# One attention and mixture-of-experts kernel: key and query splitting of the first two batches on GpSimd alone

## The chip, the cores and the metric

The kernel runs on one core of one Trainium2 chip. The metric is the device time of one execution in microseconds; the median of several runs is compared. A core has five engines with queues of their own: TensorE (matrix products; its weight loads are shown apart), VectorE, ScalarE, GpSimd and SyncE, which here issues the loads and stores. In the profile they are called PE (PEld for weight loads), DVE, ACT, POOL and SP; SPq is SP's queue.

## The reference

All data are float32. Three layers follow one another on 4 batches of 576 tokens with 8 heads of 64:

```python
scores = (q @ k.T) / 8
thresh = max(scores) - tau
scores = where(scores >= thresh, scores, -1e9)
attn = exp(scores - max(scores)); attn /= sum(attn) + 1e-9
x = attn @ v                              # heads side by side: 576 x 512

h = x.T @ U @ V                           # 576 -> 32 -> 576, over tokens
u = x + h.T
x = u + relu(u @ w_ch1) @ w_ch2           # 512 -> 2048 -> 512

e = expert of each token                  # argmax of logits, or the previous token's
out = p[e] * (relu(x @ w1[e]) @ w2[e])    # 8 experts, 512 -> 1024 -> 512
```

## The kernel before

**Split operands.** The products that must be precise are made from pairs: a high part rounded to TensorE's reduced float32 form (`F32R`) and a low part, the difference to the full value. For scores, keys are two tiles, `kh` and `kl`. The queries lie twice on the 128 partitions: in `qs`, partitions 0 to 63 hold the high part of the scaled queries and partitions 64 to 127 the low part, so that one product with `kh` and one with `kl` give the score.

**Pairs.** Heads are worked in pairs, four to a batch, numbered `i = 4 b + hp`: pairs 0 to 3 are batch 0, pairs 4 to 7 batch 1. `load_pair` (L261) loads one pair's queries and keys in pieces ("cuts"): from the second pair on, keys of 576 and 640 columns, then queries of 608 and 608. Each cut comes from memory through SP into a tile `raw` of a ring of three (L281), is copied by ScalarE into the high part (L289 keys; L292 queries, with the scale 1/8 in `t8[:, 1:2]`), and the low part is a subtraction: keys on `eng` (L290), queries on VectorE over 64 partitions (L294). `eng` is VectorE for the very first pair and for batches 2 and 3, and GpSimd otherwise. The tiles `qs`, `kh`, `kl` exist twice, so a pair's parts can be written once the scores of the pair two before it are done.

**Batch 0 alone.** `attention_alone(0)` (L553) runs first. Each of its steps takes one score tile (128 queries by 576 keys): four score products (L313, L315), the maximum on VectorE (L348), the exponential on ScalarE (L359), the thresholds (L352) and the masking with the row sum on VectorE (L363). A pair has nine such tiles. Score tiles are two in number. Beside them run the older tiles' transposes on TensorE (L416) and their copies on ScalarE (L417), the products with the values (L435, L436) and the token mixing (`chain`, L447, with `inverse`, L378, on 128x4 row sums). A generator `conv` narrows the 64-bit weights: a load `cr` (L204), a cast on ScalarE (L212), a join on VectorE (L219) and a store (L243). The next pair's `load_pair` is started during the current pair's second group, one cut a step. On TensorE a few filler products (L585) fill short steps.

**Order of the queues.** In this stage GpSimd's instructions stay in the order of the program (`tc.manual_schedule` around `attention_alone(0)`, L855). The other queues' order is laid out ahead of time by a planner, from the program's order and its own estimates of durations; instructions of later calls, such as `load_w` (L664) with its subtraction on GpSimd (L681), can stand among those of this stage.

**Later.** Batches 1 to 3 run their attention interleaved with the 512-2048-512 layer of the batch before (`channel`, L725); its weights are split by `load_w`, in batch 0's layer largely on GpSimd (L678, L681). Routing and the experts follow.

Of the kernel before, what the change touches and what calls it, by code (L numbers as in the profile page):

```python
# [8 lines left out]
F32 = mybir.dt.float32  # L9
# [5 lines left out]
AF = mybir.ActivationFunctionType  # L15
ALU = mybir.AluOpType
# [87 lines left out]
def attention_channel_moe(ctx, tc, qk, vv, tau, umat, vrep, wch, wgl, wexp, consts, out):  # L104
    nc = tc.nc
    pe, dve, act, pool, sp = nc.tensor, nc.vector, nc.scalar, nc.gpsimd, nc.sync
# [10 lines left out]
    t8 = cp.tile([128, 4], F32, name="t8")  # L117
# [135 lines left out]
    def scalars():  # L253

        sp.dma_start(out=t8[:, 0:1], in_=tau)

        dve.tensor_scalar(out=t8[:, 1:2], in0=t8[:, 0:1], scalar1=NEGTAU, scalar2=0.125, op0=ALU.is_ge, op1=ALU.mult)
        dve.tensor_scalar(out=t8[:, 2:3], in0=t8[:, 1:2], scalar1=0.0, scalar2=BIG, op0=ALU.is_equal, op1=ALU.mult)
        dve.tensor_scalar(out=t8[:, 0:1], in0=t8[:, 0:1], scalar1=0.0, scalar2=t8[:, 2:3], op0=ALU.max, op1=ALU.add)

    def load_pair(b, hp, later=None):  # L261

        i = b * NPAIR + hp
        v = ap.tile([128, VW], F32, tag="v", name=f"v{i}")
        qs = ap.tile([128, QKW], F32R, tag="qs", name=f"qs{i}")
        kh = ap.tile([128, QKW], F32R, tag="kh", name=f"kh{i}")
        kl = ap.tile([128, QKW], F32R, tag="kl", name=f"kl{i}")

        cuts = ((0, 0, 128), (1, 0, S), (0, 704, 832), (1, S, QKW), (0, 128, 704), (0, 832, QKW)) if i == 0 else (
            (1, 0, S), (1, S, QKW), (0, 0, 608), (0, 608, QKW))  # L270
        eng = dve if i == 0 or b > 1 else pool
        def steps():
            for n, (kq, c0, c1) in enumerate(cuts):
                c = slice(c0, c1)
                nm = f"raw{i}_{n}"
                if (i, n) == (0, 1):
                    x = mlp.tile([128, S], F32, tag="yr", name=nm, bufs=2)
                elif i == 0 and c1 - c0 == 128:
                    x = mlp.tile([128, 512], F32, tag="wr", name=nm, bufs=WR)
                else:  # L280
                    x = ap.tile([128, 640], F32, tag="raw", name=nm, bufs=3)  # L281
                x = x[:, :c1 - c0]
                sp.dma_start(out=x, in_=qk[i][:, kq, c])
                if (i, n) == (0, 0):
                    scalars()
                if (i, n) == (0, 3):
                    sp.dma_start(out=cst, in_=consts)
                if kq:
                    act.activation(kh[:, c], x, AF.Copy)  # L289
                    eng.tensor_tensor(out=kl[:, c], in0=x, in1=kh[:, c].bitcast(F32), op=ALU.subtract)  # L290
                else:
                    act.activation(qs[:, c], x, AF.Copy, scale=t8[:, 1:2])  # L292
                    lo, hi, xl = qs[64:128, c], qs[64:128, c].bitcast(F32), x[64:128]
                    dve.scalar_tensor_tensor(out=lo, in0=xl, scalar=t8[64:128, 1:2], in1=hi,  # L294
                                             op0=ALU.mult, op1=ALU.subtract)
                yield
            sp.dma_start(out=v, in_=vv[i])

        if later is None:
            for _ in steps():  # L300
                pass
        else:
            later.append(steps())
        return qs, kh, kl, v
# [231 lines left out]
    def attention(b):  # L536
        prev = None
        nxt = load_pair(b, 0)
        for hp in range(NPAIR):
            inp = nxt  # L540
            if hp + 1 < NPAIR:
                nxt = load_pair(b, hp + 1)
            for g in range(5):
                fr = front(b, hp, g, inp)
                yield 1.0
                if prev is not None:
                    yield from with_chain(back(*prev))
                prev = (b, hp, g, inp, fr)
        yield from with_chain(back(*prev))
        while CHAIN:  # L550
            yield link()

    def attention_alone(b):  # L553

        pend, debt, loads = [], 0.0, []
        inps = {0: load_pair(b, 0)}
        seq = [(hp, g, h) for hp in range(NPAIR) for g in range(5) for h in range(1 if g == 4 else 2)]
        groups = {}
# [816 lines left out]
```

## Time and profile before

| what | value |
|---|---|
| median of 3 runs | 1031.87 us (1031.58 to 1033.2) |
| the profiled execution's own time | 1030.82 us |
| its span, first to last instruction | 1029.0 us |
| mean granted TensorE clock | 0.997 of full |
| busy: PE, DVE, ACT, POOL | 995.0, 719.4, 612.1, 153.7 us |

The span is that of one profiled execution; 1.8 us of its time lie outside it. Busy shares are means over stages that differ: batch 0's attention alone lasts to about 100 us, batch 1's attention with batch 0's layer to about 240 us, attention altogether to about 620 us.

### The profile page before, as it was taken

The page shows a single profiled execution, that of the slowest core. Times are in us where ns is not written, and L with a number is a line of the kernel's source. Part 1 is how long each engine was busy: PE and PEld are TensorE (multiplying, and loading weights), DVE is VectorE, ACT ScalarE, POOL GpSimd, SP SyncE. Part 2 cuts the span into 40 slices and gives each one's busy share as a digit, 9 for nine tenths or more (in the row PEclk, how much of TensorE's full clock was granted, in tenths as well). Part 3 has the DMA queues.
Part 4 walks back from the last instruction along what each step waited for, and adds up shares of the span by engine and source line. Part 5 has one row for each costly group of instructions (what it writes and reads, how often), then busy time and mean ns, then how long its engine had stood idle before and what let it go on. Part 6 is the DMA issues. An engine that isn't in the chain of part 4 may idle for free.

```text
span 1029.0 us, 17858 instructions
## 1 busy us (share of the span) xinstructions
PE 995.0 (97%) x6351; PEld 835.8 (81%) x6352; DVE 719.4 (70%) x1761; ACT 612.1 (59%) x1242; POOL 153.7 (15%) x143
## 2 busy tenths in 40 slices
PE   7898999989999999999999999999999999999996
PEld 4666677768787787788888898999998988889984
DVE  7898697876778877877676664683369755576673
ACT  6888777775677777776565653422354434455562
POOL 1332245342000000000000000013400321120100
PEclk9999999999999999999999999999999999999998
DMA  6655577864323322423121111453055555556650
GB/s 215 226 145 162 164 245 254 266 205 146 118 92 94 125 71 83 127 90 94 55 68 42 42 43 31 139 208 121 25 196 178 176 201 184 173 188 199 197 184 16
DMA packets 58241, 143.72 MB, mean 140 GB/s; under 512 B 7389, under 2 KB 8157, under 8 KB 58144
## 3 DMA queue, kind: packets, MB, share of 16 engines
q1 hardware_dynamic: 54784, 132.27, 40.2%
q0 software_dynamic: 3360, 10.23, 3.1%
q8 instruction: 52, 0.85, 0.3%
q14 instruction: 45, 0.37, 0.1%
HBM read 124.65 MB, written 18.61 MB: 139 GB/s over the span
## 4 chain that ended last, share of the span: by engine, by line
PE 78%; ACT 6%; DVE 5%; DMA 5%; issue 3%; POOL 1%; SPq 0%; POOLq 0%; DVEq 0%; ACTq 0%
PE l L717 6%; PE l L719 6%; PE l L718 6%; PE l L702 6%; PE l L703 6%; PE l L704 6%; PE tp L416 4%; PE po L435 4%; PE el L1194 3%; PE el L1195 3%; PE el L1196 3%; PE s L313 3%; PE s L315 3%; PE el L1241 3%; PE el L1239 3%
## 5 line engine op out<-in xcount | busy, mean ns | idle before, releaser
L1125 ACT ACTIVATE eh<-ew 128x512 fp32r<-128x512 f32 x160 | 94.2, 628 | 67.9 <-PE el L1241 45.3
L1126 DVE TENSOR_TENSOR el<-ew,eh 128x512 fp32r<-128x512 f32 x160 | 106.6, 692 | 37.7 <-ACT eh L1125 36.3
L702 PE MATMUL l<-uh,w0h 128*128 128x256 f32 (+2 forms) x352 | 127.0, 361 | 0.3 <-ACT yT L508 0.3
L363 DVE SCALAR_TENSOR_TENSOR p<-s,st,p 128x576 f32<-128x576 f32 x144 | 114.2, 815 | 16.7 <-ACT p L359 13.1
L359 ACT ACTIVATE p<-s,st 128x576 f32<-128x576 f32 x144 | 103.8, 739 | 32.6 <-DVE st L348 31.3
L703 PE MATMUL l<-ul,w0h 128*128 128x256 f32 (+2 forms) x352 | 122.6, 348 | 0.0
L704 PE MATMUL l<-uh,w0l 128*128 128x256 f32 (+2 forms) x352 | 122.2, 347 | 0.0
L348 DVE TENSOR_REDUCE st<-s 128x1 f32<-128x576 f32 x144 | 105.2, 750 | 17.0 <-PE s L315 16.5
L717 PE MATMUL l<-hh,w1h 128*128 128x512 f32 (+3 forms) x320 | 115.2, 360 | 0.0
L719 PE MATMUL l<-hh,w1l 128*128 128x512 f32 (+3 forms) x320 | 112.9, 353 | 0.0
L718 PE MATMUL l<-hl,w1h 128*128 128x512 f32 (+3 forms) x320 | 112.2, 351 | 0.0
L417 ACT ACTIVATE ptt<-tp 128x512 f32<-128x512 f32 (+1 forms) x192 | 88.7, 491 | 30.2 <-PE tp L416 30.0
L313 PE MATMUL s<-kh,qs 128*128 128x288 f32 x320 | 95.4, 318 | 5.4 <-DVE p L363 3.5
L681 POOL TENSOR_TENSOR w1l<-wr,w1h 128x512 fp32r<-128x512 f32 x24 | 31.8, 1337 | 457.0 <-DVE rha L984 426.7
L416 PE MATMUL tp<-cst,p 128*128 128x128 f32 x576 | 90.8, 276 | 5.2 <-ACT ptt L417 5.0
L722 DVE TENSOR_TENSOR yT<-l,yT 128x448 f32<-128x448 f32 (+2 forms) x96 | 50.1, 522 | 57.9 <-PE l L719 57.5
L315 PE MATMUL s<-kl,qs 128*128 128x288 f32 x320 | 88.5, 297 | 0.0
L373 ACT ACTIVATE p<-p,rv 128x576 f32<-128x576 f32 x108 | 78.6, 771 | 16.1 <-DVE rv L380 16.0
L416 PEld LDWEIGHTS tp<-cst,p 128*128 128x128 f32 x576 | 67.8, 140 | 20.4 <-ACT ptt L417 11.4
L313 PEld LDWEIGHTS s<-kh,qs 128*128 128x128 f32 x320 | 60.3, 188 | 15.5 <-DVE p L363 6.4
L706 DVE SCALAR_TENSOR_TENSOR hl<-l,hh 128x512 fp32r<-128x512 f32 (+2 forms) x80 | 46.3, 579 | 36.7 <-ACT hh L705 36.4
L702 PEld LDWEIGHTS l<-uh,w0h 128*128 128x128 f32 x352 | 66.5, 189 | 6.8 <-DVE rsm L797 0.7
(604 smaller groups left out, 2473.0 us busy)
## 6 DMA issues: line engine op xcount, KB each, us to landing
ew<-in_wexp_dram SPq DMA_DIRECT2D x80, 512.0 KB, 4.6
wr<-wdram SPq DMA_DIRECT2D x128, 256.0 KB, 3.1
cr<-in_wch_dram SPq DMA_DIRECT2D x32, 512.0 KB, 5.1
raw<-in_qk_dram SPq DMA_DIRECT2D x30, 304.0 KB, 3.2
wdram<-w SPq DMA_DIRECT2D x32, 256.0 KB, 3.0
v<-in_vv_dram SPq DMA_DIRECT2D x16, 352.0 KB, 4.1
raw<-in_qk_dram SPq DMA_DIRECT2D x16, 320.0 KB, 3.6
raw<-in_qk_dram SPq DMA_DIRECT2D x17, 288.0 KB, 3.3
```

The costliest lines, as they stand in the source:

```text
L313: pe.matmul(s["t"][:, h, :288], lhsT=qs[:, qc:qc + 128], rhs=kh[:, k0:k0 + 288], start=(j == 0), stop=False)
L315: pe.matmul(s["t"][:, h, :288], lhsT=qs[:, qc:qc + 128], rhs=kl[:, k0:k0 + 288], start=False, stop=(j == n - 1))
L348: dve.tensor_reduce(out=self.st[:, 0, h:h + 1], in_=self.t[h], axis=AX.XY, op=ALU.max, negate=True)
L363: dve.scalar_tensor_tensor(out=p, in0=self.t[h], scalar=self.st[:, 1, h:h + 1], in1=p, op0=ALU.is_ge, op1=ALU.mult, accum_out=self.rvs[:, ...
L416: pe.transpose(tp[:, c - c0], src[:, c * 128:c * 128 + 128], ident)
L702: pe.matmul(pm, lhsT=w1h[:, wk], rhs=uh[k], start=(k == 0), stop=False)
L703: pe.matmul(pm, lhsT=w1h[:, wk], rhs=ul[k], start=False, stop=False)
L704: pe.matmul(pm, lhsT=w1l[:, wk], rhs=uh[k], start=False, stop=(k == 3))
L717: pe.matmul(pm, lhsT=w2h[:, wd], rhs=xh, start=(f == f0), stop=False)
L718: pe.matmul(pm, lhsT=w2h[:, wd], rhs=xl, start=False, stop=False)
L719: pe.matmul(pm, lhsT=w2l[:, wd], rhs=xh, start=False, stop=(f == f0 + 3))
L1126: dve.tensor_tensor(out=lo, in0=x, in1=hi.bitcast(F32), op=ALU.subtract)
```

## The change

For pairs 1 to 7 the high parts of the keys are copied by GpSimd instead of ScalarE; their low parts were on GpSimd already. For pairs 1 to 3 GpSimd takes the queries as well: it scales the raw cut in place, copies it into the high part, and subtracts on the 64 lower partitions. Pair 0 and the queries of pairs 4 to 7 stay as they were, and so do batches 2 and 3.

```diff
         eng = dve if i == 0 or b > 1 else pool
+        own = eng is pool
...
                 if kq:
-                    act.activation(kh[:, c], x, AF.Copy)
+                    if own:
+                        pool.tensor_copy(kh[:, c], x)
+                    else:
+                        act.activation(kh[:, c], x, AF.Copy)
                     eng.tensor_tensor(out=kl[:, c], in0=x, in1=kh[:, c].bitcast(F32), op=ALU.subtract)
+                elif own and b == 0:
+                    lo, hi, xl = qs[64:128, c], qs[64:128, c].bitcast(F32), x[64:128]
+                    pool.tensor_scalar(out=x, in0=x, scalar1=t8[:, 1:2], scalar2=None, op0=ALU.mult)
+                    pool.tensor_copy(qs[:, c], x)
+                    pool.tensor_tensor(out=lo, in0=xl, in1=hi, op=ALU.subtract)
                 else:
                     act.activation(qs[:, c], x, AF.Copy, scale=t8[:, 1:2])
                     lo, hi, xl = qs[64:128, c], qs[64:128, c].bitcast(F32), x[64:128]
```

## Rows read from the trace of the kernel before

**Rows 1.** The page: busy us, share of the span and instructions of each engine.
```profile
PE 995.0 (97%) x6351; PEld 835.8 (81%) x6352; DVE 719.4 (70%) x1761; ACT 612.1 (59%) x1242; POOL 153.7 (15%) x143
```
**Rows 2.** Busy time by stage: stretch, its length, busy us and instructions by engine, clock, DMA.
```profile
10.00:98.00 88.00, 75.82 (x529) 54.98 (x530) 80.57 (x194) 71.09 (x148) 24.34 (x20) 1.00 0.60 182
...
120.00:240.00 120.00, 114.56 (x689) 88.20 (x688) 95.43 (x193) 88.11 (x166) 49.48 (x48) 1.00 0.79 249
```
**Rows 3.** Waits of VectorE, 10 to 98 us: total us, times, longest.
```profile
DVE st L348 <- PE s L315: 3.4, 6, 1.2
DVE p L363 <- ACT p L359: 2.2, 3, 1.1
```
**Rows 4.** Waits of TensorE, 10 to 98 us.
```profile
PE tp L416 <- ACT ptt L417: 4.1, 6, 1.5
```
**Rows 5.** ScalarE's groups, 10 to 98 us: busy us, mean ns | idle before.
```profile
L292 ACT ACTIVATE qs<-raw,t 128x608 fp32r<-128x608 f32 x8 | 6.5, 810 | 1.6 <-DMA raw<-in_qk_dram 1.6
...
L289 ACT ACTIVATE kh<-raw 128x640 fp32r<-128x640 f32 x5 | 3.7, 739 | 0.7 <-DMA raw<-in_qk_dram 0.7
L289 ACT ACTIVATE kh<-raw 128x576 fp32r<-128x576 f32 x5 | 3.4, 681 | 1.4 <-issue 0.8 <-POOL w1l L681 0.6
```
**Rows 6.** VectorE in order of time: start us, duration us, instruction, idle before.
```profile
18.52 0.85 DVE L294 SCALAR_TENSOR_TENSOR qs<-raw,t,qs 64x608 fp32r<-64x608 f32 x1
...
38.68 0.82 DVE L363 SCALAR_TENSOR_TENSOR p<-s,st,p 128x576 f32<-128x576 f32 x1 [1.09 <-ACT p L359]
...
46.99 0.16 DVE L379 TENSOR_SCALAR rv<-rv 128x4 f32<-128x4 f32 x1
...
51.36 1.02 DVE L379 TENSOR_SCALAR rv<-rv 128x4 f32<-128x4 f32 x1
...
79.43 0.85 DVE L294 SCALAR_TENSOR_TENSOR qs<-raw,t,qs 64x608 fp32r<-64x608 f32 x1
```
**Rows 7.** ScalarE in order of time.
```profile
14.71 0.69 ACT L289 ACTIVATE kh<-raw 128x576 fp32r<-128x576 f32 x1
...
19.84 0.80 ACT L292 ACTIVATE qs<-raw,t 128x608 fp32r<-128x608 f32 x1 [0.35 <-DMA raw<-in_qk_dram]
...
37.22 0.80 ACT L292 ACTIVATE qs<-raw,t 128x608 fp32r<-128x608 f32 x1 [0.79 <-DMA raw<-in_qk_dram]
```
**Rows 8.** Waits of TensorE, 118 to 245 us.
```profile
PE tx L461 <- ACT yT L442: 2.7, 3, 1.1
```
**Rows 9.** VectorE's groups, 10 to 98 us.
```profile
L294 DVE SCALAR_TENSOR_TENSOR qs<-raw,t,qs 64x608 fp32r<-64x608 f32 x8 | 7.5, 935 | 0.3
...
L219 DVE SCALAR_TENSOR_TENSOR w<-cr,top 128x512 int32<-128x512 int32 x7 | 6.4, 912 | 0.0
L379 DVE TENSOR_SCALAR rv<-rv 128x4 f32<-128x4 f32 x8 | 3.8, 478 | 0.1
...
L219 DVE SCALAR_TENSOR_TENSOR wv<-crv,top 128x512 int32<-128x512 int32 x1 | 0.7, 684 | 0.0
```
**Rows 10.** GpSimd's groups, 10 to 98 us.
```profile
L290 POOL TENSOR_TENSOR kl<-raw,kh 128x640 fp32r<-128x640 f32 x5 | 8.2, 1647 | 0.1
L290 POOL TENSOR_TENSOR kl<-raw,kh 128x576 fp32r<-128x576 f32 x5 | 7.5, 1494 | 18.4 <-ACT kh L289 18.4
...
L678 POOL CAST w1h<-wr 128x512 fp32r<-128x512 f32 x1 | 0.6, 610 | 16.0 <-DMA wr<-wdram 16.0
```
**Rows 11.** TensorE in order of time.
```profile
28.61 0.38 PE L313 MATMUL s<-kh,qs 128*128 128x288 f32 x1
```
**Rows 12.** GpSimd in order of time.
```profile
51.06 1.28 POOL L681 TENSOR_TENSOR w1l<-wr,w1h 128x512 fp32r<-128x512 f32 x1 [2.01 <-ACT w1h L680]
```
**Rows 13.** SyncE's queue in order of time: DMA issues.
```profile
18.52 3.62 SPq L283 DMA_DIRECT2D raw<-in_qk_dram  x3
23.86 7.05 SPq L204 DMA_DIRECT2D cr<-in_wch_dram  x3
```
**Rows 14.** Waits of ScalarE, 10 to 98 us.
```profile
ACT top L212 <- DMA cr<-in_wch_dram: 0.2, 1, 0.2
```

## The prediction, made before the changed kernel was run

> **What bounds the kernel now.** I read the page first: TensorE is busy 97% of the span, VectorE 70%, ScalarE 59%, GpSimd 15% [rows 1]. That is an average over unlike stages, so the table of windows comes next [rows 2]. In the second attention stage (120 to 240 us) TensorE works 114.6 of 120 us and little is left to win. In the first batch's attention alone, which runs steadily from 10 to 98 us, VectorE is the fullest: 80.6 of 88 us (92%), TensorE 75.8 (86%), ScalarE 71.1 (81%), GpSimd 24.3 (28%). What VectorE waits for there is short: 3.4 us for scores and 2.2 us for the exponential [rows 3]; TensorE's longest wait is 4.1 us for ScalarE's copies of the transposed probabilities [rows 4]. So this stage is paced by VectorE, with ScalarE and TensorE close behind, and it is worth what VectorE's queue gets shorter, as long as the others can follow. Behind it lies TensorE work of a fixed size, so I let a gain of this stage arrive at the end whole.
>
> **Removed from ScalarE.** In the stage, ten key copies (five pairs, the next batch's first two among them) of 739 and 681 ns, 7.1 us, and six query copies of 810 ns, 4.9 us: 12.0 us, to 59 us [rows 5]. ScalarE is not the fullest engine, so I give this no price by itself; it shows only where ScalarE holds up others. At 37.22 a query copy stood 0.79 us at the head of ScalarE's queue for its load; the exponential behind it came late, and VectorE idled 1.09 us before its mask at 38.68 [rows 6, 7]. That wait goes to GpSimd's queue: minus 1.1 us. Shorter queues should trim TensorE's 4.1 us as well [rows 4], which come back as VectorE's 3.4 us for scores; I take 0.5 us. Four more key copies (pairs 6 and 7, 2.8 us) fall into 120 to 240 us, where TensorE's longest wait on ScalarE is 2.7 us in three pieces [rows 8]; I take nothing there, with 2.7 as the far end.
>
> **Removed from VectorE.** Eight query subtractions of 64x608 stand in the stage, 7.5 us [rows 9]; the two of pair 4 (the first at 79.43, 0.85 us) stay [rows 6], so six leave, 5.8 us.
>
> **Added to GpSimd.** A 128x512 cast there takes 0.61 us, a two-input subtraction 1.49 (576 columns) and 1.65 (640) [rows 10]. Scaled by columns, a key copy is 0.69 or 0.76 and a query copy 0.72; the query subtraction 1.57, taken as one of 608 columns, though it covers 64 partitions. A scaling with a per-partition factor has no row on GpSimd: from below the cast, 0.72, from above the two-input subtraction, 1.57. It reads one tensor, as the cast does, so I take 0.72. A query cut is then 3.0 us (3.9), a pair's keys 1.45 more. In the stage: 6 x 3.0 + 5 x 1.45 = 25.3 us, GpSimd from 24.3 to 49.6 of some 84 us (59%); it does not become the bound.
>
> **Is it in time?** Pair 1 is the tightest. Its first key copy stood at 14.71 and its last query load had landed by 19.84 [rows 7]. From 14.7 GpSimd's chain is 0.7 + 1.5 + 0.8 + 1.65 (19.3), first query cut 22.3, second 25.3 (27.1 with the dear scaling). TensorE's first scores of pair 1 start at 28.61 [rows 11]. Hidden, by 3 us and more; uncovered, each late microsecond would cost one on TensorE and so on all.
>
> **The shared reads.** VectorE's small 128x4 scaling took 0.16 us at 46.99, with GpSimd idle, but 1.02 at 51.36 [rows 6]: GpSimd's 1.28 us subtraction had begun at 51.06 and ended at 52.34, and VectorE's ended at 52.38 [rows 12]. It waited the other's instruction out. Groups hit so: the 128x4 scalings, 8 x (478 - 160) = 2.5 us, the two-input joins, 7 x (912 - 684) = 1.6, and the query subtractions, 8 x (935 - 850) = 0.7 [rows 6, 9]. The first two, 4.1 us, stay exposed. If VectorE arrives at a random moment it waits half of the instruction that it meets, so the sum grows with the squares of GpSimd's durations: now 24.7 us2 for ten key subtractions and about 12 for the other 8.6 us; added 5 for key copies, 21 for query cuts; over 84 instead of 88 us that is a factor 1.8. So 4.1 becomes 7.4: plus 3.3 us (plus 4.7 with the dear scaling; nothing, if arrivals happen to miss).
>
> The Trainium skill (SBUF — State Buffer, Who interferes with whom) calls the port pair of VectorE and GpSimd an exclusive lock: the later of the two blocks for the whole instruction if the VectorE one uses a 2-port mode or two SBUF inputs. The trace agrees with it in the 1.02 us above. A reader who left the lock out would book 5.8 + 1.1 + 0.5 = 7.4 us of gain; with it the sum is 4.1.
>
> **Sum.** Minus 5.8, plus 3.3, minus 1.1, minus 0.5: minus 4.1 us. The profiled execution took 1030.82 us (span 1029.0); the median of the runs is 1031.87, 1.05 above. So 1031.87 - 4.1 = 1027.8 us. What a measurement of this kernel can tell from no change is 0.2%, 2.1 us.
>
> **Rivals.**
> *Same: VectorE's freed time turns into waiting.* TensorE, at 75.8 of 88 us, could close in at once, and most of the net 2.5 us on VectorE would return as longer waits for the other two; also the dear scaling leaves only 5.8 - 4.7 + 1.6 = 2.7 us, and a little less is within the noise. Against: VectorE's waits for both others are 5.6 of 88 us now, ScalarE gets 12 us lighter and TensorE has 12 us of room [rows 2, 3]. Time 1031 (1030 to 1033).
>
> *Slower: VectorE waits out GpSimd.* The 15 exposed instructions wait 0.79 us each if they always meet a two-input GpSimd instruction at a random moment, which is 11.8 us and only eats the gain (1031.87 - 5.8 + 7.7 - 1.6 = 1032.2). If they become ready just as GpSimd starts, as at 51.36, where 0.86 of 1.28 us was waited, they wait up to 1.57 each. At 1.1 us, 16.5 in all, it is plus 12.4: 1031.87 + 12.4 - 7.4 = 1036.9 (1044 with all waits whole). Behind the waiting instruction stand maximum and mask, and behind them TensorE's next scores. It makes the kernel slower by 0.2% once the stalls pass 4.1 + 7.4 + 2.1 = 13.6 us. For it: GpSimd at 59%. Against: that is not always, and half of the added instructions are of some 0.7 us.
>
> *Slower: raw buffers held longer.* Three raw buffers feed SyncE's queue. Pair 2's three loads were issued over 3.6 us from 18.52 as buffers came free, and the three weight loads of the conversion stand right behind at 23.86 [rows 13]. GpSimd frees the first query buffer at 22.3, where VectorE did at 19.4 [rows 6]. Up to 3 us per pair could pass to the weight loads, whose casts sit in ScalarE's ordered queue before exponentials: 3 x 3 - 4.1 = 5 us slower, 1036.5, from the point where the casts' loads have no lead left. Against: ScalarE's wait on those loads is 0.2 us in the whole stage [rows 14].
>
> *Queues laid differently.* Only GpSimd's order is written out in this stage; subtractions of a later call already stand among the first batch's at 51.06 [rows 12]. A changed step can reorder the rest, by some 2 us either way; it is no part of the sum.
>
> *More than forecast.* If stalls don't grow and both of VectorE's waits shrink [rows 3]: minus 5.8 - 2.2 - 1 = 9, 1022.9.
>
> **How the numbers follow.** Forecast (2 to 7 us gained) 0.57; more than that 0.05; same 0.19; VectorE waiting out GpSimd 0.09; raw buffers 0.04; reordered to worse 0.06 (1034 to 1036). Faster by over 0.2%: 0.57 + 0.05 = 0.62; within: 0.19; slower: 0.19. The range takes in 1022.5 (the gain without stalls) and reaches to 1033.7 (just under what 0.2% calls slower, 1034); the forecast's own is 1024.5 to 1029.8.
>
> **What would show it.** Right: no query subtraction of pairs 1 to 3 on VectorE, GpSimd near 50 us busy in the stage, 128x4 scalings and joins with a mean near 0.6 and 1.0 us, pair 4's first scores some 4 us earlier, and the same lead at 240 us. A query scaling near 1.5 us would halve the gain. Wrong: TensorE waiting on GpSimd's query parts; ScalarE's casts waiting for weight loads; stalls over 13.6 us; or a lead after the stage that is gone at 240.

## The result and the profile after

The changed kernel is slower. Its median is 1044.53 us (1042.07 to 1047.67, four runs) against 1031.75 us for the kernel before on the same chip (1031.58 to 1033.2): a ratio of 1.0118, interval 1.0097 to 1.0139. The forecast was 1027.8, range 1022.5 to 1033.7; direction and range were both missed. The profiled execution took 1045.72 us, its span is 1043.7, 14.7 us more than before. Lines move by 1 to 9 after the change: L284 loads `raw`, L291 and L294 are the key copy and subtraction on GpSimd, L297 to L299 the three new query instructions, L682 loads the weights `wr`, L689 and L690 copy and subtract them.

The first line of the page, which answers to [rows 1]:

```profile
PE 1001.6 (96%) x6352; PEld 841.1 (81%) x6352; DVE 713.4 (68%) x1755; ACT 601.4 (58%) x1222; POOL 190.8 (18%) x175
```

The table of windows, with columns as in [rows 2]; the last two rows cut the first batch's stage finer:

```profile
10.00:98.00 88.00, 70.29 (x460) 50.80 (x461) 68.20 (x173) 55.69 (x117) 50.82 (x42) 0.94 0.56 176
66.00:76.00 10.00, 2.49 (x31) 1.93 (x29) 2.59 (x7) 1.85 (x7) 1.29 (x2) 0.79 0.54 173
76.00:86.00 10.00, 9.68 (x51) 7.60 (x52) 7.25 (x18) 6.89 (x15) 5.77 (x5) 0.70 0.36 91
```

VectorE's 80.6 us in the first stage became 68.2, so work left the fullest engine as intended, and GpSimd's 24.3 became 50.8, as worked out. But TensorE fell from 75.8 to 70.3: the stage did not run faster on a lighter VectorE, it did less in the same time. The row of 66 to 76 us says where: no compute engine was busy for more than 2.6 of 10 us.

How far each kernel is shows in the start of the first maximum of a pair's scores (VectorE's timeline, L348 before, L357 after) and of ScalarE's first copy into `uh` (after batch 0) and into `rest` (after batch 1), in us:

| kernel | pair 2 | pair 3 | pair 4 | after batch 0 | after batch 1 | span |
|---|---|---|---|---|---|---|
| before | 53.2 | 76.5 | 100.8 | 102.9 | 236.8 | 1029.0 |
| after | 50.3 | 83.4 | 109.5 | 112.8 | 248.7 | 1043.7 |
| after, pair 4's loads later | 50.7 | 76.7 | 101.4 | 104.7 | 241.6 | 1035.3 |
| the same, change in batch 0 alone | 50.3 | 73.5 | 101.4 | 103.9 | 238.1 | 1030.9 |

(The last two are experiments below.) The changed kernel is 2.9 us ahead at pair 2, as forecast, and 6.9 us behind at pair 3: a swing of 9.8 us inside one pair. It loses 1.8 more by pair 4, 3.2 more to the end of batch 1 and 2.8 behind it. Single executions differ already at the start: in those of kernels whose first two pairs are as before, pair 1 begins between 30.4 and 33.8 us. A lead of 1 or 2 us is therefore better read from pair to pair: from pair 1's first maximum to pair 2's it is 22.7 us before and 20.2 after.

The chain of work that ended last, through that place (start, us, what):

```profile
67.02 0.43 DVE st L357
67.45 3.47 DMA wdram<-w
70.94 4.03 DMA wr<-wdram
75.01 0.51 issue
75.52 0.58 ACT ptt L426
76.32 0.80 PE rep L500 x2
```

The wait is for a weight block that is stored to memory and loaded back. ScalarE in order of time:

```profile
74.98 0.63 ACT L689 ACTIVATE w1h<-wr 128x512 fp32r<-128x512 f32 x1 [8.15 <-DMA wr<-wdram]
75.52 0.58 ACT L426 ACTIVATE ptt<-tp 128x512 f32<-128x512 f32 x1
76.00 0.27 ACT L496 ACTIVATE tT<-tT 128x128 f32<-128x128 f32 x1
76.16 0.74 ACT L368 ACTIVATE p<-s,st 128x576 f32<-128x576 f32 x1
```

VectorE and TensorE at the same place:

```profile
76.93 0.82 DVE L372 SCALAR_TENSOR_TENSOR p<-s,st,p 128x576 f32<-128x576 f32 x1 [7.73 <-ACT p L368]
```

```profile
67.86 0.30 PE L324 MATMUL s<-kl,qs 128*128 128x288 f32 x1
68.00 0.49 PE L425 MATMUL tp<-cst,p 128*128 128x128 f32 x3
76.32 0.80 PE L500 MATMUL rep<-tT,cst 128*128 128x128 f32 x2 [7.83 <-ACT tT L496]
...
78.22 0.44 PE L324 MATMUL s<-kl,qs 128*128 128x288 f32 x1
```

A weight copy stands 8.15 us at the head of ScalarE's ordered queue. Behind it stand a transposed copy, a mixing copy and an exponential whose inputs had long been there; VectorE waits 7.73 us for the exponential and TensorE 7.83 us for the mixing copy. Then TensorE itself is slower: a score product takes 0.44 us where it took 0.30 before the stop. Its granted clock fell during the stop, in which it did next to nothing for some 8 us, and stood at the lower of its two levels (1.2 of 2.4 GHz) from about 72 to 82 us; the mean from 76 to 86 us is 0.70 of full.

Why the block came late stands in SyncE's queue. First before the change, then after:

```profile
60.23 0.33 SPq L243 DMA_DIRECT2D wdram<-w  x1
...
63.30 0.33 SPq L283 DMA_DIRECT2D raw<-in_qk_dram  x1
63.75 0.35 SPq L673 DMA_DIRECT2D wr<-wdram  x1
```

```profile
55.31 6.72 SPq L284 DMA_DIRECT2D raw<-in_qk_dram  x3
...
67.06 0.33 SPq L284 DMA_DIRECT2D raw<-in_qk_dram  x1
67.45 0.43 SPq L243 DMA_DIRECT2D wdram<-w  x1
...
70.94 0.33 SPq L682 DMA_DIRECT2D wr<-wdram  x1
```

The store that the load needs left at 60.23 before and at 67.45 after; the load went out 7.2 us later. Two things came together. Pair 4's third `raw` load stood behind the store before (63.30); the planner has now put it in front (67.06). And there it had to wait for a buffer. The loads ahead of it were out by 62.03, so in the order of before the store could have followed some 5 us earlier (an estimate). GpSimd in order of time shows who held the buffer:

```profile
61.77 1.81 POOL L297 TENSOR_SCALAR raw<-raw,t 128x608 f32<-128x608 f32 x1
63.56 1.27 POOL L690 TENSOR_TENSOR w0l<-wr,w0h 128x512 fp32r<-128x512 f32 x1
64.78 0.69 POOL L298 CAST qs<-raw 128x608 fp32r<-128x608 f32 x1
65.55 1.49 POOL L299 TENSOR_TENSOR qs<-raw,qs 64x608 fp32r<-64x608 f32 x1
```

The subtraction ends at 67.04 and the load goes out at 67.06. The three instructions of one query cut, with a weight subtraction between them, held the buffer 5.3 us. The Trainium skill (DMA: Bandwidth & Descriptors, Anatomy of one DMA — SWDGE (gpsimd) path) says that a transfer's wait happens on the issuing sequencer before dispatch; the trace agrees for SyncE, where the store stood behind a waiting load: with that load placed later it left at 58.57 (below).

### The profile page after: what moved, and what is told of

Same layout as the page of the kernel before. It is cut to its first block, busy times and chain, and to the rows that moved or that the text cites. A ratio compares the mean times of both kernels' runs of the same rounds, so it can differ in the third digit from the quotient of the medians.

```text
span 1043.7 us, 17874 instructions
## 1 busy us (share of the span) xinstructions
PE 1001.6 (96%) x6352; PEld 841.1 (81%) x6352; DVE 713.4 (68%) x1755; ACT 601.4 (58%) x1222; POOL 190.8 (18%) x175
## 4 chain that ended last, share of the span: by engine, by line
PE 74%; DMA 8%; ACT 6%; DVE 5%; issue 3%; POOL 3%; SPq 0%; POOLq 0%; DVEq 0%; ACTq 0%
PE l L726 6%; PE l L728 6%; PE l L727 6%; PE l L711 5%; PE l L712 5%; PE l L713 5%; PE po L444 4%; PE tp L425 4%; PE el L1203 3%; PE el L1204 3%; PE el L1205 3%; PE s L322 3%; PE el L1250 3%; PE el L1248 3%; PE s L324 3%
## 5 line engine op out<-in xcount | busy, mean ns | idle before, releaser
L357 DVE TENSOR_REDUCE st<-s 128x1 f32<-128x576 f32 x144 | 105.2, 749 | 19.8 <-PE s L324 18.8
L690 POOL TENSOR_TENSOR w1l<-wr,w1h 128x512 fp32r<-128x512 f32 x24 | 31.6, 1326 | 457.0 <-DVE rha L993 426.7
L444 PE MATMUL po<-ptt,v 128*64 128x256 f32 (+1 forms) x256 | 71.8, 419 | 3.3 <-ACT ptt L433 2.7
L445 PE MATMUL po<-ptt,v 128*64 128x256 f32 (+1 forms) x256 | 72.1, 419 | 0.5 <-ACT ptt L426 0.4
```

The lines of the kernel that those rows point to most:

```text
L444: pe.matmul(po[:64, :n], lhsT=v[:, j * 64:j * 64 + 64], rhs=ptt[:, j], start=(j == 0), stop=False)
```

## Experiments

Two theories were put against each other from the first runs on. A: GpSimd holds the `raw` buffers longer, SyncE's queue waits for them, a weight load behind is late, and ScalarE's ordered queue stands. B: the added GpSimd instructions themselves slow VectorE through the shared reads, whatever buffers they hold. Runs went to chips on which the kernel before had medians from 1031.5 to 1036.3 us, so each is told as the ratio to the kernel before on its own chip.

**One part of the change at a time.** Without the query branch (`keys_only`), and without the key copies (`queries_only`):

```diff
-                elif own and b == 0:
+                elif False:
```
```diff
-                    if own:
+                    if False:
```

> The change's key part alone (queries again on ScalarE and VectorE). Theory A, raw buffers: GpSimd holds the query cuts for three instructions, 4 us each, so SyncE's ordered queue stands still, the weight load behind it comes late and ScalarE stands before it; without the queries no such stop, 1030 to 1033 us. Theory B, shared reads: VectorE waits out GpSimd's instructions, in proportion to GpSimd's added 25 us, of which 7 are left: some 3.5 us slower, 1035.

> The change's query part alone (key copies again on ScalarE). Theory A: the stop of about 8 us is there, 1039 to 1046 us. Theory B: 18 of the 25 us of GpSimd's added work, about 9 us slower, 1041. It tells the theories apart only together with the keys alone.

The keys alone gave 1.0083 (1.0057 to 1.0109), the queries alone 1.0092 (1.0062 to 1.0122), where the whole change gave 1.0118. The parts don't add up. With the queries alone ScalarE's weight copy waited 5.7 us, as A says. For the keys alone both theories expected less; where that loss lies was not settled.

**The weight copies on another queue.** `load_w` copies the first two weight blocks on ScalarE. Here GpSimd takes them, on the changed kernel (`w_pool`) and on the one before (`before_w_pool`):

```diff
-            if b == 0 and f > 1:
+            if b == 0:
```

> The whole change, and the high parts of the first two weight blocks of the first layer copied by GpSimd, so that ScalarE no longer stands before that load. Theory A: the weight load comes as late as before, but GpSimd waits for it and the 8.1 us of ScalarE's wait, with the clock's drop behind it, are gone: 1031 to 1037 us. Theory B: GpSimd has 2.5 us more to do, so 1044 to 1046.

> Control: the kernel before, with those same four weight copies on GpSimd. Theory A: ScalarE's wait for weights is 0.8 us there, so nothing to win, 1030 to 1033 us. Theory B: 2.5 us more on GpSimd, 1032 to 1033.

On the kernel before it did nothing: 1.0006 (0.9992 to 1.002). On the changed one the ratio was still 1.0088 (1.0053 to 1.0123), and the stop had moved. GpSimd, SyncE and ScalarE in order of time:

```profile
80.21 0.61 POOL L687 CAST w1h<-wr 128x512 fp32r<-128x512 f32 x1 [9.42 <-DMA wr<-wdram]
```
```profile
84.84 1.82 SPq L284 DMA_DIRECT2D raw<-in_qk_dram  x3
```
```profile
87.73 0.80 ACT L301 ACTIVATE qs<-raw,t 128x608 fp32r<-128x608 f32 x1 [6.30 <-DMA raw<-in_qk_dram]
```

Now GpSimd's own ordered queue stands 9.42 us before the weight copy; the key cuts behind it free `raw` late, and ScalarE waits 6.30 us for a query load. The late weight load holds up whichever ordered queue has its copy. That speaks for A's origin, in SyncE's queue, and shows that ScalarE is only where it came out.

**The added instructions without the move.** The kernel before with the added GpSimd instructions as extra work of 576 columns whose results nobody uses. In `scratch` they read a tile of ones; in `hold` the same lines read `x[:, :S]`, the `raw` cut, and so hold its buffer as well. The copies for the key cuts run in batch 1 too, and the results lie in the rings of `hh` and `hl`, which batch 0's layer also uses:

```diff
+                    if b < 2 and i:
...
+                        pool.tensor_copy(y2, scr)
...
+                    if b == 0 and i:
+                        z = scr
...
+                        pool.tensor_scalar(out=y1, in0=z, scalar1=t8[:, 1:2], scalar2=None, op0=ALU.mult)
+                        pool.tensor_copy(y2, z)
+                        pool.tensor_tensor(out=y1[64:128], in0=z[64:128], in1=y2[64:128].bitcast(F32), op=ALU.subtract)
```

> The kernel before, with the change's extra GpSimd work done besides, on a tile of ones that no load waits for (576 columns a cut): scaling, copy and subtraction per query cut, one copy per key cut. Nothing is taken from ScalarE or VectorE, and no raw buffer is held longer. Theory A (raw buffers held by GpSimd stop SyncE's queue): 1031 to 1034 us. Theory B (VectorE waits out GpSimd): the stalls grow by 4 us or more without any relief, 1036 to 1042.

> The same extra GpSimd work, but reading the raw cuts themselves, so that each raw buffer is free only when GpSimd is through; ScalarE and VectorE still do the real work. Theory A: SyncE stands before the loads as in the changed kernel, 1040 us or more. Theory B: as with the tile of ones, to within 2 us.

`scratch` gave 1.007 (1.0047 to 1.0094) and `hold` 1.0029 (1.0011 to 1.0047). So extra GpSimd work costs without the move; but holding the buffer added nothing in this layout, against A in its simplest form. SyncE and ScalarE of `hold` show why:

```profile
62.56 4.67 SPq L283 DMA_DIRECT2D raw<-in_qk_dram  x2
67.29 0.42 SPq L243 DMA_DIRECT2D wdram<-w  x1
...
70.81 0.33 SPq L683 DMA_DIRECT2D wr<-wdram  x1
```
```profile
73.95 0.63 ACT L690 ACTIVATE w1h<-wr 128x512 fp32r<-128x512 f32 x1
```

The weight load goes out as late as in the changed kernel, at 70.81. But here the copy's turn in ScalarE's queue comes only at 73.95, and it waits for nothing: without the relief this kernel is at pair 2 only at 56.2, and its queue is laid otherwise. Between these two kernels the late load costs the one in which its consumer already stands at the head of an ordered queue; the relief of VectorE brought that moment forward. In `scratch` two of VectorE's groups answer to [rows 9]:

```profile
L299 DVE SCALAR_TENSOR_TENSOR qs<-raw,t,qs 64x608 fp32r<-64x608 f32 x8 | 9.9, 1235 | 0.3
L221 DVE SCALAR_TENSOR_TENSOR w<-cr,top 128x512 int32<-128x512 int32 x6 | 6.2, 1038 | 0.0
```

The query subtractions took 1235 ns instead of 935 and the joins 1038 instead of 912: 8 x 0.30 + 6 x 0.13 = 3.2 us. That is less than half of 0.7%; the 128x4 scalings fell meanwhile, from 478 to 254 ns, and the subtractions are the very instructions that the change removes. More of the loss lies behind the stage: from pair 4's first maximum to the first copy into `rest`, `scratch` takes 141.4 us, the kernel before 136.0. ScalarE in that stretch:

```profile
192.61 0.80 ACT L297 ACTIVATE qs<-raw,t 128x608 fp32r<-128x608 f32 x1 [4.75 <-DMA raw<-in_qk_dram]
```

TensorE waits 4.79 us behind it, and its mean granted clock is 0.83 from 190 to 200 us, where it was 1.00 before. So `scratch`, which holds no `raw` cut by its added work, shows a wait for a query load like those that A names, and doesn't speak for B alone. Why `hold` cost less was not settled.

**The late copy taken out of ScalarE's way.** `late_w` puts the four ScalarE weight copies of the first two blocks behind the last value copy of batch 0 (`MARK0`); `late_w1` only the two of the second halves (`elif b == 0 and i == 1`); `before_late_w1` is the same edit on the kernel before:

```diff
+            elif b == 0:
+                with tc.issue_after(MARK0[0]):
+                    act.activation(hi, x, AF.Copy)
             else:
                 act.activation(hi, x, AF.Copy)
```

> The whole change, with ScalarE's copies of the first two weight blocks of the next layer put behind the first batch's last value copy, so that ScalarE does not stand before the weight load in the stage. Theory A: the 8.1 us of that wait go, and the clock's drop with it: 1030 to 1036 us. Theory B: unchanged, 1042 to 1046.

> The whole change; of ScalarE's weight copies only the two second-layer halves, which are needed last, are put behind the first batch's last value copy. Theory A, now in this form: the loss is ScalarE standing before copies whose loads come late because SyncE's queue waits for raw buffers on GpSimd. Then taking the one copy that stood 8.1 us out of the stage brings back about 9 us, without the 5 us that the later start of the next layer cost when all four were put off: 1032 to 1036 us. Theory B, shared reads: 1043 to 1046.

> Control: the kernel before, with the two second-layer weight copies of ScalarE put off as in the other runs. Theory A: nothing waits there for these loads, so 0.998 to 1.002. If putting off helps by itself, below 0.998, and the change would still cost something.

`late_w` 1.0031 (1.0013 to 1.005), `late_w1` 1.0037 (1.0016 to 1.0058): some 70% of the loss gone. But the putting off costs by itself: the control gave 1.0034 (1.0019 to 1.0048). Against it, the change under `late_w1` costs nothing that can be told. ScalarE's standing queue was the main way in which the loss arrived.

**The order in SyncE's queue alone.** This is the decisive pair. `p4_late` leaves every computation of the changed kernel as it is and places only pair 4's `raw` loads behind pair 3's value load; `before_p4_late` does the same to the kernel before:

```diff
-                sp.dma_start(out=x, in_=qk[i][:, kq, c])
+                with tc.issue_after(VL[3]) if i == 4 else nullcontext():
+                    sp.dma_start(out=x, in_=qk[i][:, kq, c])
...
-            sp.dma_start(out=v, in_=vv[i])
+            VL[i] = sp.dma_start(out=v, in_=vv[i]).ins
```

> The whole change; only on SyncE's queue, the raw loads of pair 4 (the first of batch 1) are put behind the value load of pair 3, so that the weight store and load of the second block no longer stand behind a raw load that waits for GpSimd. No computing instruction is altered. Theory A, in full (SyncE's queue stands before raw buffers that GpSimd holds): ScalarE's 8.1 us wait for the weight load shrinks to 2 us or less, 1032 to 1037 us by the scale of the first runs, ratio 1.000 to 1.005. Rival: the load is late for another reason (the store's data, DMA engines busy): ratio 1.010 or more.

> Control: the kernel before, with pair 4's raw loads behind pair 3's value load on SyncE's queue. Theory A: nothing there waits on these loads, so a ratio of 0.998 to 1.002, and the gain of the same step under the change (0.7%) is the change's own loss. If the order helps by itself, it is below 0.998.

`p4_late` gave 1.0048 (1.0033 to 1.0064), the control 1.0007 (0.9993 to 1.0021). So the order is worth nothing to the kernel before, and gives the changed one back 1.18 - 0.48 = 0.70%, some 7 us. (The planner kept the order of the control's compute queues; in `p4_late` a few instructions change places from 64 us on, among them ScalarE's weight copy, which stands six instructions earlier. The 7 us are the worth of the order with what the planner made of it.) SyncE and ScalarE in `p4_late`:

```profile
58.57 0.33 SPq L243 DMA_DIRECT2D wdram<-w  x1
...
60.90 0.32 SPq L685 DMA_DIRECT2D wr<-wdram  x1
```
```profile
64.54 0.63 ACT L692 ACTIVATE w1h<-wr 128x512 fp32r<-128x512 f32 x1 [0.33 <-DMA wr<-wdram]
```

The store leaves 8.9 us earlier, the copy waits 0.33 instead of 8.15 us, and pair 3 starts at 76.7 instead of 83.4.

**More room for the buffers.** In `k0_yr` the first key cut of each pair of batches 0 and 1 goes to the other ring that pair 0 uses, so that `raw` is one cut less loaded:

```diff
-                if (i, n) == (0, 1):
+                if b < 2 and kq and c1 - c0 == S:
```

> The whole change, with the first key cut of each pair of batches 0 and 1 loaded into another, idle pair of tiles, so that the ring of three raw buffers serves three cuts instead of four. Theory A: SyncE waits less for raw buffers, and the weight load goes out earlier: 1031 to 1038 us, unless the planner places the next loads so much earlier that they wait again. Theory B: 1043 to 1046.

1.0079 (1.0051 to 1.0107), and ScalarE's weight copy waited 9.7 us: the next loads were laid out earlier too and waited again in front of it. One cut less on the ring is no cure here: the loads that follow come up in the queue earlier and wait there.

**The loads on GpSimd's own queue.** `pool_loads` issues the `raw` loads of pairs 1 to 7 from GpSimd, one cut ahead, so that they can't stand before SyncE's weight transfers:

```diff
+                pool.dma_start(out=xs[n], in_=qk[i][:, kq, c0:c1])
...
-                sp.dma_start(out=x, in_=qk[i][:, kq, c])
+                if not own:
+                    sp.dma_start(out=x, in_=qk[i][:, kq, c])
```

> The whole change, with the raw cuts of pairs 1 to 7 loaded from GpSimd's own queue, one cut ahead, so that SyncE's queue never waits for a raw buffer of these pairs. Theory A: SyncE's weight loads and stores go out on time and the stop is gone; GpSimd pays some 1 us per load: 1028 to 1035 us. Theory B: unchanged or worse, 1043 to 1050.

1.025 (1.0206 to 1.0293), by far the worst. GpSimd's groups, 10 to 98 us (busy us, mean ns, idle before):

```profile
L279 POOL DMA_DIRECT2D raw<-in_qk_dram x19 | 10.9, 572 | 17.0 <-DVE qs L317 9.6 <-DVE st L375 7.1 <-POOL qs L313 0.3
```

Each issue takes GpSimd 572 ns, and its queue now stands 17.0 us in this stage before a load that has to wait, with the cuts behind it. The wait in front of a load was moved, not removed.

**Batch 0 and batch 1 apart.** The change for batch 0 alone, plain, with the late copies, and with the late loads (`b0_only`, `b0_late_w1`, `b0_p4_late`):

```diff
-        own = eng is pool
+        own = eng is pool and b == 0
```

> The change for batch 0 alone (pairs 1 to 3); the keys of pairs 4 to 7 are copied by ScalarE again. Theory A: the 8 us stop lies in batch 0 and stays, the 2 us that batch 1's stretch became longer go: 1040 to 1043 us. Theory B: 10 of 35 us of GpSimd's added work are gone: 1040 to 1042.

> Batch 0 alone and the two second-layer weight copies put off. Theory A: what is left of the change is its relief on VectorE and ScalarE: 1028 to 1033 us. Theory B: 1040 to 1042.

> The change for batch 0 alone, with pair 4's raw loads put behind the value load of pair 3. Theory A: what is left is the relief, a ratio of 0.996 to 1.001. Rival: 1.008, as for batch 0 alone.

Plain it gave 1.0085 (1.0068 to 1.0101) with the weight copy waiting 8.2 us; with the late copies 1.0004 (0.9988 to 1.002), where the control `before_late_w1` costs 1.0034; with the late loads 0.9985 (0.9972 to 0.9999), the one version that came out under the kernel before. In both of the latter pair 3 starts 3.0 to 3.5 us earlier than in the kernel before (73.5 and 73.0 against 76.5): that is the forecast's relief. 2.5 us of it are won inside pair 1 and 0.2 to 0.7 inside pair 2; the rest lies before them. The windows of `b0_p4_late` answer to [rows 2], and its waits of VectorE, 10 to 98 us, to [rows 3]:

```profile
10.00:98.00 88.00, 76.40 (x533) 55.11 (x533) 75.17 (x187) 64.35 (x137) 53.17 (x44) 0.98 0.59 183
80.00:86.00 6.00, 5.72 (x27) 3.22 (x29) 4.02 (x9) 3.81 (x10) 0.00 (x0) 0.72 0.54 158
```

```profile
DVE p L375 <- ACT p L371: 6.4, 9, 1.7
DVE st L360 <- PE s L327: 4.3, 8, 1.8
```

TensorE does 76.4 us in the first stage, little more than before, on a VectorE 5.4 us lighter: VectorE now waits 10.7 us for the other two, where it waited 5.6. Of the 3.0 us at pair 3 nothing is left at pair 4 (101.4 against 100.8). Part of that has a place in the trace: at 78.15 a query copy of pair 4 waits 0.84 us for its load, TensorE waits 1.88 us for a copy behind it, and from 80 to 86 us its clock is 0.72, where it was 1.00 before. `b0_late_w1` waits at the same place, ScalarE 2.20 and TensorE 2.51 us, without a fall of the clock.

And the key copies of batch 1 alone, on the kernel before (`b1_only`):

```diff
-                    act.activation(kh[:, c], x, AF.Copy)
+                    if b == 1:
+                        pool.tensor_copy(kh[:, c], x)
+                    else:
+                        act.activation(kh[:, c], x, AF.Copy)
```

> The key copies of pairs 4 to 7 alone on GpSimd, batch 0 as before. By the differences of the runs with and without this part (1.0118 against 1.0085, 1.0048 against 0.9985) a ratio of 1.003 to 1.006. If its cost exists only together with batch 0's part: 0.999 to 1.001.

1.0067 (1.0039 to 1.0094). From the other side, `p4_late` and `b0_p4_late` of one chip differ in nothing else: 1.0048 - 0.9985 = 0.63%. Two more pairs of runs that differ in this part alone give half of it: the whole change and `b0_only`, 1.0118 - 1.0085 = 0.33%, and `late_w1` and `b0_late_w1`, 1.0037 - 1.0004 = 0.33%. So batch 1's eight key copies cost 0.33 to 0.67%, some 3.4 to 6.9 us, depending on what else is laid around them; the forecast had booked them at nothing. ScalarE in order of time, 97 to 245 us, its longest waits for query loads, in `p4_late` and then in `b0_p4_late`:

```profile
102.86 0.80 ACT L304 ACTIVATE qs<-raw,t 128x608 fp32r<-128x608 f32 x1 [2.03 <-DMA raw<-in_qk_dram]
187.71 0.80 ACT L304 ACTIVATE qs<-raw,t 128x608 fp32r<-128x608 f32 x1 [2.12 <-DMA raw<-in_qk_dram]
```
```profile
185.29 0.80 ACT L304 ACTIVATE qs<-raw,t 128x608 fp32r<-128x608 f32 x1 [0.89 <-DMA raw<-in_qk_dram]
```

TensorE of `p4_late` behind them:

```profile
104.20 0.33 PE L428 MATMUL tp<-cst,p 128*128 128x128 f32 x1 [1.60 <-ACT ptt L429]
...
189.47 0.48 PE L447 MATMUL po<-ptt,v 128*64 128x320 f32 x1 [2.18 <-ACT ptt L436]
```

It looks like the first stop in small: a query load waits for a `raw` buffer that GpSimd's key cut frees, its copy stands in ScalarE's ordered queue for 2 us, and TensorE waits 1.6 and 2.2 us for copies behind it. `after` has the first of the two as well (a wait of 1.99 us at 110.94, TensorE 1.57) and so has `b1_only` (1.84 and 1.53 us). TensorE's two waits add up to 3.8 us. Behind the second its mean granted clock is 0.83 from 190 to 200 us, in `b0_p4_late` 1.00: another 1.7 us of its work (10 x 0.17, an estimate). The cost is shown, by four comparisons; the cause is likely, not shown: kernels without these copies can wait there too. `scratch` did (4.75 us, above), and so did the profiled execution of `before_p4_late`, which took 7.5 us more than that kernel's median: 3.64 us at 190 us, with a clock of 0.66 from 190 to 200.

## Why the prediction was wrong

**The step that failed** is the rival "raw buffers held longer", in its place and its price, together with "queues laid differently", which stood beside it as another case. The two came at once: GpSimd held a buffer 5.3 us, and the planner had put the load that waited for it in front of a store. They were given 4 and 6 in 100, and the second was booked at some 2 us. The prediction had the start of it right: three `raw` buffers, a query cut that frees one later, weight transfers behind in SyncE's queue, copies in ScalarE's ordered queue before exponentials. What it set against it was ScalarE's wait of 0.2 us on the `cr` loads [rows 14]. Those are the loads of raw 64-bit weights. The load that came late was another, `wr`, the joined weights that are stored and loaded back, and that block has two places in the same queue, a store and a load: held once, it pays the delay and then the whole way through memory, 3.47 + 4.03 us in the chain. The trace before had the sign in SyncE's own waits, 10 to 98 us (total us, times, longest), which the prediction did not read:

```profile
SPq L283 <- POOL kl L290: 24.4, 8, 9.4
```

`raw` loads already stood 24.4 us for buffers that GpSimd's key subtractions held. The question should have been what lies behind such a load if it waits 5 us, for every kind of transfer in that queue. The price was 3 us a pair (9 - 4.1 on the median gives 1036.8, not the 1036.5 written); it was one stop of 8.15 us, and after it slow products at the lower clock.

**Minus 5.8, minus 1.1, minus 0.5: the work left, the waits did not.** In `b0_p4_late`, without the stop, VectorE is 5.4 us lighter, and the stage is 3.0 us ahead at pair 3. But the two waits of VectorE that were to shrink grew from 5.6 to 10.7 us, and at pair 4 the lead is gone. Even without the stop the runs thus show less than the sum of 4.1: 0.15%, some 1.5 us, and most of the way the rival "Same", VectorE's freed time turned into waiting. Pair 1 was in time, as worked out: its first maximum starts at 30.1 against 30.4.

**Plus 3.3 for the shared reads: too dear.** GpSimd's groups of the changed kernel, 10 to 98 us, then VectorE's:

```profile
L297 POOL TENSOR_SCALAR raw<-raw,t 128x608 f32<-128x608 f32 x6 | 10.9, 1819 | 0.3
L299 POOL TENSOR_TENSOR qs<-raw,qs 64x608 fp32r<-64x608 f32 x6 | 9.2, 1536 | 0.5
...
L298 POOL CAST qs<-raw 128x608 fp32r<-128x608 f32 x6 | 4.2, 692 | 0.3
```
```profile
L219 DVE SCALAR_TENSOR_TENSOR w<-cr,top 128x512 int32<-128x512 int32 x6 | 4.9, 820 | 0.0
...
L388 DVE TENSOR_SCALAR rv<-rv 128x4 f32<-128x4 f32 x7 | 2.2, 313 | 0.1
```

The means fell, from 478 to 313 and from 912 to 820 ns: 7 x 0.15 + 6 x 0.14 = 1.9 us, where the forecast had 7.4. Part of the stage is the stop, in which nothing can collide; `b0_p4_late`, which has none, shows 8 scalings of 384 and 7 joins of 946 ns, 8 x 0.22 + 7 x 0.26 = 3.6 us. Outside these groups three single instructions of the start grew there, by 1.3 us together (the cast into `vst` from 418 to 1032 ns, the joins into `wv` and `wu` by 246 and 456). So the stalls of the named groups did not grow with GpSimd's busy time, 24 to 53 us, and with these three they grew by 0.8 us, not 3.3; that they grow with the squares of its durations did not hold here. What meets what must then hang on how the queues are laid; that was not tried by itself. The rival built on the same stalls, 1036.9, is out as the main cause: the order of some loads would not have given 7 us back.

**The scaling** lies outside its bounds, 0.72 to 1.57 us: 1819 ns. It read one tensor, yet cost more than the subtraction of two. A query cut is 1.82 + 0.69 + 1.54 = 4.05 us, not 3.0, which is a good third more of buffer time; GpSimd's total of 50 us came out nonetheless, since pair 5's key instructions no longer fell into the stage.

**Batch 1's keys at nothing: wrong.** The cover named was TensorE's short waits on ScalarE [rows 8]. But the copies cost 3.4 to 6.9 us, by four comparisons. That the copy, in leaving ScalarE, moved the moment at which `raw` is freed is the likely reason, not a shown one; the waits of 3.8 us and the lower clock behind them are what the trace gives a place to.

**The sum as it ran.** Of 1.18%, 0.70 is the place of pair 4's loads, 0.63 is batch 1's keys, and minus 0.15 is what is left of the change in batch 0 without either. The parts overlap: taken in the other order, batch 1's keys are 0.33 (the whole change against `b0_only`) and the place of the loads 1.00 (`b0_only` against `b0_p4_late`).

## What to carry to other kernels

When a step moves to a slower engine, price not only its busy time but how long it now holds its input buffer; then read, in the queue that issues the loads, every transfer that stands behind the next load into that buffer, and for each of these, which ordered compute queue has its consumer ahead of other work. Where a planner lays the queues out, that order can change with the step: compare it too. A wait of before that is short says nothing about the transfer next to it: ask each for its lead. Here moving one group of loads behind another in the issue order was worth 7 us to the changed kernel and nothing to the one before.

## What the runs showed of the hardware

- On GpSimd the scaling by a per-partition factor took 1819 ns for 128x608 (1806 to 1931 in other runs), the plain cast of the same size 692, the two-input subtraction on 64 partitions 1536.
- A stop of some 8 us on TensorE was followed by products at 0.44 instead of 0.30 us and a mean granted clock of 0.70 from 76 to 86 us; in the same stage before, the clock was 1.00 [rows 2]. Waits of 1.88 us (`b0_p4_late`) and 2.18 us (`p4_late`) were followed by a mean of 0.72 over 80 to 86 us and 0.83 over 190 to 200; one of 2.51 us (`b0_late_w1`) was not, the clock stayed at 1.00.
- A load issued from GpSimd's queue took 572 ns of that engine's time; one `raw` load issued from SyncE's took 0.33 us.
